# S4D convolution beside a gated linear unit: squarings two at a time, another order in the preparation, other stores

## The chip, the cores and the metric

The kernel runs on one core of one Trainium2 chip. The metric is the device time of one execution in microseconds (us); the time before the change is the median of three runs, 716.96 us. The engines are named as in the profile: PE is TensorE, DVE is VectorE, ACT is ScalarE, POOL is GpSimd and SP is SyncE, which issues most DMAs.

## The reference

The input x is 1 x 2048 x 448 (L positions, D channels), N = 256 modes per channel, and the hidden width of the gated unit is 1792. All is fp32.

```python
xn = (x - mean) / sqrt(var + 1e-5)                   # over the channels
dt = exp(log_dt); A = -exp(log_A_real) + 1j*A_imag; C = (C_real + 1j*C_imag) * dt
P  = exp((A*dt)[:, :, None] * arange(L))             # D x N x L
K  = 2 * einsum("dn,dnl->dl", C, P).real
y  = irfft(rfft(xn.T, 2L) * rfft(K, 2L))[:L].T + xn * D_skip
h  = sigmoid(xn @ w_gate) * (xn @ w_up)
out = x + y + h @ w_down
```

## The kernel before, in words

Two Python generators write the program: `conv` (L1016), the long convolution, and `glu` (L727), the gated unit. A loop at the end (L1106 to L1125) takes the next piece from the one that is behind by its planned share of the work (`WP`, `WX`, `WK`, `WS` are planned costs). The tile framework then schedules the instructions of each engine; `tc.issue_after(ins)` keeps an instruction behind `ins` in that order, and `hp` gives priority. Each engine runs its own row of instructions in order.

The gated unit. The hidden width is cut in 14 pieces of 128, and positions in tiles of 512. An fp32 product is done as three products of high and low parts (`xh`, `xl`; `wh`, `wl`; `hh`, `hl`; `dh`, `dl`). For each piece and tile `gate` (L692) makes two halves `gu` in PSUM (L706, 12 matmuls each), ACT makes `th` (L714), DVE `hf` from `th` and the second half (L717), ACT `hh` (L722), DVE `hl` (L724). So hf is what frees the banks of `gu`. DVE also makes `wl` from the loaded weights (L760). After a group of pieces the down projection `po` runs (L819) and DVE adds it into `acc` (L824). The banks with the tag "gu" are four, in turn, for gate halves, `po`, `kq` and the transposes of x (L212), whose low parts DVE takes out as `xl` (L222) and `xr` (L225); `xr` holds the last 64 channels, high and low.

The convolution's stages:
- Layer norm (statistics L248 to L263, `xn` L270) and transposes, to about 30 us.
- `prep` (L342), run as two generators for the two halves of the channels: `exp` (L304) with the fractions `fr` (L312, L313) and a polynomial `pl` (L317), reciprocals in pieces of 128 columns (`pieces`, L321 to L323), `m`, `w`, `s` (L368 to L372). A round of both generators is placed behind the hf that is `LAG` = 3 hfs back. The layer norm statistics of the second 8 blocks of x stand in the program ahead of these rounds, behind `xls[0]`, the instruction that makes `xr` of the second tile of x. `x_spec` (matmuls L281) makes spectra of x between rounds.
- `kgen` (L458), 107 to 535 us: 56 chunks of 8 channels in 7 groups of 8. Per chunk PE makes phases `tr` (L539), ACT sines `S` (L545 to L548), POOL multiplies magnitudes `me`, `mf` (L517) out of powers `pm`, ACT squares some (L530), DVE makes `Et` (two products, L599 and L600) and `Ft` (L601), and PE multiplies them into `ko` (64 matmuls, L613). `powers` (L446) makes the `pm` of the next group: ten squarings on DVE (L453), three copies with 1 added on ACT (L451, L456). It is called once a group, at its chunk c = 4, behind the Ft of the chunk before.
- `spectra` (L841), 535 to 700: products with tables (`there`, `back`, L900 and L927), and inverse transforms `last(h, m)` (L960) that DVE adds into the outputs (L968). h is the half of the channels; m = 0, 2, 4, 6 stands for pairs of blocks of both halves of the output. They are interleaved with the end of the gated unit.

Stores: `out` (L234) writes four blocks of half width for four partition groups, each on the next of the queues of SP, ACT and POOL in turn. The first two quarters of the output lie in `ac`, the last two in `accs[2]` and `accs[3]`. In the last group of the gated unit `last(1, 0)` and `last(1, 2)` come ahead of the third block of the second tile, `last(1, 4)` and `last(1, 6)` behind the fourth.

## Time and profile before

| | |
|---|---|
| runs | 716.56, 716.96, 721.07 us; median 716.96 |
| profiled execution | 717.89 us; span 716.1 us; mean granted clock 0.98 |
| PE busy | 671.3 us, 94% |
| DVE busy | 550.8 us, 77% |
| ACT busy, POOL busy | 428.7 us, 378.8 us |
| DMA | 117.22 MB, mean 164 GB/s |

The profile is of one execution. The span runs from its first instruction to its last; the execution's own time has 1.8 us more. A row of the time line has the start in us, the busy time in us, the engine, the line, the operation with output and inputs, and how many were put together; in square brackets stands the engine's idle time just before, and what ended it. Rows of one engine overlap a little, since they are pipelined, so what one costs is better seen from start to start. A row of the table by windows has busy time (and count of instructions) of PE, PE's weight loads, DVE, ACT and POOL, then the clock granted to PE as a share of full speed, the DMA share and GB/s. Line numbers are those of the kernel before, unless rows of the order after are shown, whose numbers differ by 1 to 5.

### The profile page before, as it was taken

Reading aid. Unit: us, or ns where it says so; the run is one execution under the profiler, and the core shown is the slowest. Engines: PE = TensorE matmul, PEld = TensorE weight load, DVE = VectorE, ACT = ScalarE, POOL = GpSimd, SP = SyncE. Lnnn points to the kernel's source line nnn. Section 1 sums busy time; section 2 is a strip of 40 time slices with the busy share of each in tenths; the row PEclk is TensorE's granted clock in tenths of the full one; section 3 lists DMA queues with packets and bytes.
Section 4 is the critical chain, followed back from the end, with each engine's and each line's share of the span. In section 5 each row is a group of like instructions: output and inputs, shape, how many; then the busy total and the mean of one; then the engine's idle time right before and its main releaser. Section 6 shows DMA issues by size and latency. Waiting matters only on the chain.

```text
span 716.1 us, 19096 instructions
## 1 busy us (share of the span) xinstructions
PE 671.3 (94%) x7752; PEld 528.2 (74%) x7752; DVE 550.8 (77%) x766; ACT 428.7 (60%) x678; POOL 378.8 (53%) x431
## 2 busy tenths in 40 slices
PE   3898999999997998999999999999989999999995
PEld 2676888878876885656878778887867777776784
DVE  5899997599889889898588988987936555556543
ACT  3656974588687689996578778678643322313320
POOL 2101138556987978797368688598954002351002
PEclk9998999999999898999999999999999999999998
DMA  9947174464254444556933333242259988999645
GB/s 204 235 145 231 50 230 132 145 198 136 63 169 148 138 111 127 160 164 196 274 107 101 95 110 116 68 147 57 57 173 309 242 234 239 264 281 222 182 131 154
DMA packets 93991, 117.22 MB, mean 164 GB/s; under 512 B 12240, under 2 KB 77776, under 8 KB 93904
## 3 DMA queue, kind: packets, MB, share of 16 engines
q1 hardware_dynamic: 65904, 91.87, 45.6%
q10 hardware_dynamic: 25424, 18.24, 8.8%
q0 software_dynamic: 2576, 5.90, 2.9%
q8 instruction: 61, 1.00, 0.6%
q14 instruction: 26, 0.21, 0.1%
HBM read 72.13 MB, written 43.84 MB: 162 GB/s over the span
## 4 chain that ended last, share of the span: by engine, by line
PE 71%; DVE 13%; ACT 4%; issue 3%; SPq 3%; DMA 3%; POOL 1%; ACTq 0%; POOLq 0%; DVEq 0%
PE gu L706 29%; PE po L819 17%; PE sp L900 7%; PE ko L613 6%; PE pv L927 4%; PE tr L539 4%; SPq L489 2%; DVE Et L599 1%; PE gu L281 1%; DVE Ft L601 1%; DVE Et L600 1%; DMA acc<-in_A_u_dram 1%; DMA ph<-ph_d 1%; DVE pm L453 1%; DVE hl L724 1%
## 5 line engine op out<-in xcount | busy, mean ns | idle before, releaser
L517 POOL TENSOR_TENSOR me<-me,pm 128x32 f32<-128x32 f32 (+1 forms) x168 | 145.1, 864 | 67.6 <-DVE Et L600 56.8
L517 POOL TENSOR_TENSOR mf<-mf,pm 128x64 f32<-128x64 f32 (+1 forms) x112 | 121.3, 1083 | 6.1
L706 PE MATMUL gu<-xh,wh 128*128 128x512 f32 x336 | 100.5, 406 | 0.7 <-ACT xh L221 0.7
L706 PE MATMUL gu<-xh,wl 128*128 128x512 f32 x336 | 96.2, 393 | 0.0
L706 PE MATMUL gu<-xl,wh 128*128 128x512 f32 x336 | 96.1, 392 | 0.0
L600 DVE TENSOR_TENSOR Et<-me,S 128x1024 f32<-128x1024 f32 x56 | 79.7, 1423 | 14.4 <-ACT me L530 14.0
L599 DVE TENSOR_TENSOR Et<-me,S 128x1024 f32<-128x1024 f32 x56 | 79.1, 1414 | 14.3 <-ACT S L548 13.6
L819 PE MATMUL po<-dh,hh 128*128 128x448 f32 x224 | 85.0, 379 | 2.9 <-DVE hf L717 2.9
L601 DVE TENSOR_TENSOR Ft<-mf,S 128x1024 f32<-128x1024 f32 x56 | 80.1, 1430 | 6.5 <-PE ko L613 4.0
L819 PE MATMUL po<-dl,hh 128*128 128x448 f32 x224 | 83.1, 371 | 0.0
L819 PE MATMUL po<-dh,hl 128*128 128x448 f32 x224 | 81.8, 369 | 0.0
L545 ACT ACTIVATE S<-tr 128x1024 f32<-128x1024 f32 x56 | 57.9, 1034 | 37.8 <-PE tr L539 36.1
L613 PEld LDWEIGHTS ko<-Et,Ft 128*32 128x32 f32 x3584 | 55.5, 112 | 30.6 <-issue 13.6
L706 PEld LDWEIGHTS gu<-xh,wh 128*128 128x128 f32 x336 | 61.7, 191 | 19.8 <-issue 4.4
L613 PE MATMUL ko<-Et,Ft 128*32 128x64 f32 x3584 | 66.5, 224 | 9.4 <-DVE Ft L601 7.4
L722 ACT CAST hh<-hf 128x512 fp32r<-128x512 f32 x56 | 35.0, 625 | 65.6 <-DVE hf L717 58.3
L706 PEld LDWEIGHTS gu<-xh,wl 128*128 128x128 f32 x336 | 63.4, 189 | 14.4 <-DVE hf L717 0.7
L706 PEld LDWEIGHTS gu<-xl,wh 128*128 128x128 f32 x336 | 63.4, 189 | 13.5
L783 POOL TENSOR_TENSOR dl<-rd,dh 128x448 fp32r<-128x448 f32 x14 | 26.2, 1871 | 83.5 <-ACT dh L782 83.5
L548 ACT ACTIVATE S<-S,hpi 128x1024 f32<-128x1024 f32 x56 | 65.7, 1174 | 0.0
L824 DVE SCALAR_TENSOR_TENSOR acc<-po,acc 128x448 f32<-128x448 f32 x80 | 48.0, 615 | 21.1 <-PE po L819 21.0
L717 DVE SCALAR_TENSOR_TENSOR hf<-th,gu 128x512 f32<-128x512 f32 x56 | 38.0, 679 | 32.1 <-PE gu L706 24.5
(208 smaller groups left out, 1302.1 us busy)
## 6 DMA issues: line engine op xcount, KB each, us to landing
sk_d<-sk ACTq DMA_DIRECT2D x14, 512.0 KB
sx<-x_d SPq DMA_DIRECT2D x32, 224.0 KB
skl<-sk_d SPq DMA_DIRECT2D x16, 448.0 KB
vp<-v_d SPq DMA_DIRECT2D x16, 448.0 KB
v_d<-vt SPq DMA_DIRECT2D x14, 448.0 KB
ph<-ph_d SPq DMA_DIRECT2D x224, 24.0 KB
wt_d<-wh SPq DMA_DIRECT2D x9, 512.0 KB
wt_d<-wl SPq DMA_DIRECT2D x9, 512.0 KB
```

The costliest lines, as they stand in the source:

```text
L517: ins = nc.gpsimd.tensor_tensor(m[:, :, w + a : 2 * w : n], m[:, :, a:w:n], par(base + i).unsqueeze(2).to_broadcast([128, 4 * DC, w // n]) ...
L545: nc.scalar.activation(rows(cs), pv, AF.Abs)
L548: sins[:] = [nc.scalar.activation(cs, cs, AF.Sin, scale=-TWO_PI, bias=hpi)]
L599: v.tensor_tensor(Et[:, :, :, 32:64], two(me[:, :, 32:64]), S[:, 1::-1], ALU.mult)
L600: v.tensor_tensor(Et[:, :, :, 0:32], two(me[:, :, 0:32]), S[:, 1:3, :, ::-1], ALU.mult)
L601: fts[:] = [v.tensor_tensor(Ft, two(mf), S[:, 3:5], ALU.mult)]
L613: mm = nc.tensor.matmul(ko[32 * j : 32 * j + 32, sl], Ft[:, cc, DC * h + 4 * q + j], Et[:, cc, DC * h + 4 * q + j], start=(k == 0), stop=( ...
L706: glu_mm[:] = [nc.tensor.matmul(ps, a_, b_, start=(n == 0), stop=(n == len(mm) - 1))]
L717: marks[1] = v.scalar_tensor_tensor(hf, th, 1.0, pgu[1], ALU.add, ALU.mult)
L819: glu_mm[:] = [nc.tensor.matmul(po, a_[:, bs], w_, start=(n == 0), stop=(n == 3 * fc - 1))]
L824: v.scalar_tensor_tensor(acc[:, b], po, 0.5, acc[:, b], ALU.mult, ALU.add)
L900: mm = nc.tensor.matmul(to, tb[:kk, t, 64 * c : 64 * c + 64], rhs, start=True, stop=True, skip_group_check=True,)
```

## The change

Three things are changed; what is computed is not.

**Squarings.** `powers` takes a list of the squarings to make, and is called at chunks c = 1 to 6 of a group instead of once at c = 4: two squarings a chunk by a table of numbers, at c = 6 all three ACT copies and no squaring. Each call stands behind the Ft of the chunk before.

**Preparation.** The first two rounds of `prep` (exponent clamp, fractions) are as before; rounds after the second are also behind `xls[0]`, and the statistics of the second 8 blocks come after the third round, behind `frs[0]`, the last of the fractions (L313). `x_spec` comes one round later.

**Stores.** `out` is given the queues, the columns and the number of blocks. The first half of the columns of `ac` and of `accs[2]` goes on POOL's queue only, the second on SP's and ACT's. In the last group `last(1, 4)` and `last(1, 6)` come ahead of the fourth block of the second tile instead of behind it, with stores of `accs[2]`'s second half and of blocks 12 to 14 at full width; after the fourth block only block 15 is stored.

```diff
+PWS = [(), (1, 2), (3, 4), (5, 7), (8, 9), (10, 11), (12,)]
...
-    def out(src, b0, h):
-        ds = slice(H * h, H * h + H)
+    def out(src, b0, nb, ds, engs):
         for g in range(4):
-            eng = (nc.sync, nc.scalar, nc.gpsimd)[outs[0] % 3]
-            outs[0] += 1
-            eng.dma_start(blocks(out_t, g, b0, 4)[:, :, ds], src[32 * g : 32 * g + 32, :, ds])
+            eng = engs[g % len(engs)]
+            eng.dma_start(blocks(out_t, g, b0, nb)[:, :, ds], src[32 * g : 32 * g + 32, b0 % 4 : b0 % 4 + nb, ds])
...
-        v.scalar_tensor_tensor(fr, ki, -ln2l, fr, ALU.mult, ALU.add)
+        frs[:] = [v.scalar_tensor_tensor(fr, ki, -ln2l, fr, ALU.mult, ALU.add)]
...
-    def powers(pms, g, behind=None):
+    def powers(pms, g, js=range(1, 13), behind=None):
...
-        with tc.issue_after(behind.ins) if behind else nullcontext():
-            nc.scalar.activation(pm[:, 0], w, AF.Identity, bias=one)
-        for j in (1, 2, 3, 4, 5, 7, 8, 9, 10, 11):
-            v.scalar_tensor_tensor(pm[:, j], w, 2.0, w, ALU.add, ALU.mult)
-            w = pm[:, j]
-        for o in (slice(1, 6), slice(7, 12)):
-            nc.scalar.activation(pm[:, o], pm[:, o], AF.Identity, bias=one)
+        for j in js:
+            if j in (6, 12):
+                continue
+            src = w if j == 1 else pm[:, j - 2 if j == 7 else j - 1]
+            v.scalar_tensor_tensor(pm[:, j], src, 2.0, src, ALU.add, ALU.mult)
+        if js[-1] == 12:
+            with tc.issue_after(behind.ins) if behind else nullcontext():
+                nc.scalar.activation(pm[:, 0], w, AF.Identity, bias=one)
+                for o in (slice(1, 6), slice(7, 12)):
+                    nc.scalar.activation(pm[:, o], pm[:, o], AF.Identity, bias=one)
...
-                if c == 4 and NCH * (g + 1) < NCK:
+                if 0 < c < 7 and NCH * (g + 1) < NCK:
                     with tc.issue_after(fts[0].ins):
-                        powers(pms, g + 1, sins[0])
+                        powers(pms, g + 1, PWS[c], sins[0])
...
-                        if final and (t, b) == (1, 2):
+                        if final and t == 1 and b >= 2:
                             sp_mm[:] = glu_mm
-                            for m in (0, 2):
+                            for m in (4 * b - 8, 4 * b - 6):
                                 lasts[0](1, m)
+                            if b == 3:
+                                out(accs[2], 8, 4, slice(H, D), (nc.sync, nc.scalar))
+                                out(accs[3], 12, 3, slice(0, D), (nc.sync, nc.scalar))
...
-                    if final:
-                        out(acc, 8 + 4 * t, 0)
-                if final:
-                    sp_mm[:] = glu_mm
-                    for m in (4, 6):
-                        lasts[0](1, m)
-                    for t in range(2):
-                        out(accs[2 + t], 8 + 4 * t, 1)
+                    if final and t == 0:
+                        out(acc, 8, 4, slice(0, H), (nc.gpsimd,))
+                    elif final:
+                        out(acc, 15, 1, slice(0, D), (nc.sync, nc.scalar))
...
-                    out(ac[:, 4 * q : 4 * q + 4], 4 * q, h)
+                    out(ac[:, 4 * q : 4 * q + 4], 4 * q, 4, ds, (nc.sync, nc.scalar) if h else (nc.gpsimd,))
...
-                with tc.issue_after(xls[0].ins):
-                    for b in range(8):
-                        x_stats(sm, 8 + b, xes[b // 4][:, b % 4])
-                x_scales(sm, 8, 8)
...
                     for p in list(preps):
                         try:
-                            with tc.issue_after(hfs[max(0, len(hfs) - LAG)].ins):
+                            behind = tc.issue_after(xls[0].ins) if n > 1 else nullcontext()
+                            with tc.issue_after(hfs[max(0, len(hfs) - LAG)].ins), behind:
                                 next(p)
...
+                    if n == 2:
+                        with tc.issue_after(frs[0].ins):
+                            for b in range(8):
+                                x_stats(sm, 8 + b, xes[b // 4][:, b % 4])
+                        x_scales(sm, 8, 8)
...
-                    if n in (2, 3):
+                    if n in (3, 4):
```

What stands in DVE's row at three places. First, from the second hf on (about 29.6 us before): the fractions `fr`, the low parts `xl` and `xr`, and the first statistics. Before:

```order
L717 SCALAR_TENSOR_TENSOR hf<-th,gu 128x512
L312 SCALAR_TENSOR_TENSOR fr<-ki,ex 112x514 x2
L222 TENSOR_TENSOR xl<-tr,xh 128x512
L313 SCALAR_TENSOR_TENSOR fr<-ki,fr 112x514
L222 TENSOR_TENSOR xl<-ko,xh 128x512
L313 SCALAR_TENSOR_TENSOR fr<-ki,fr 112x514
L222 TENSOR_TENSOR xl<-kp,xh 128x512
L225 TENSOR_TENSOR xr<-gu,xr 64x512
L248 BN_STATS st_84<-xe_116 128x6 x4
```

and after:

```order
L719 SCALAR_TENSOR_TENSOR hf<-th,gu 128x512
L223 TENSOR_TENSOR xl<-tr,xh 128x512
L223 TENSOR_TENSOR xl<-ko,xh 128x512
L223 TENSOR_TENSOR xl<-kp,xh 128x512
L226 TENSOR_TENSOR xr<-gu,xr 64x512
L311 SCALAR_TENSOR_TENSOR fr<-ki,ex 112x514 x2
L726 TENSOR_TENSOR hl<-hf,hh 128x512
L312 SCALAR_TENSOR_TENSOR fr<-ki,fr 112x514 x2
L247 BN_STATS st_84<-xe_116 128x6 x4
```

The four passes for the fractions went from ahead of `xr` to behind it.

Second, some rows on, from the fourth hf back to the reciprocals. Before, from the fourth hf:

```order
L717 SCALAR_TENSOR_TENSOR hf<-th,gu 128x512
L368 SCALAR_TENSOR_TENSOR m_379<-a_377,b_378 112x512
L370 TENSOR_TENSOR w_380<-a_377,b_378 112x512
L372 TENSOR_TENSOR s_381<-a_377,b_378 112x512
L368 SCALAR_TENSOR_TENSOR m_391<-a_389,b_390 112x512
L370 TENSOR_TENSOR w_392<-a_389,b_390 112x512
L372 TENSOR_TENSOR s_393<-a_389,b_390 112x512
...
L323 RECIPROCAL m_379<-m_379 112x128 x2
L724 TENSOR_TENSOR hl<-hf,hh 128x512
L323 RECIPROCAL m_379<-m_379 112x128 x2
L323 RECIPROCAL m_391<-m_391 112x128
```

and after, up to the fourth hf (the third stands 16 rows ahead of it):

```order
L367 SCALAR_TENSOR_TENSOR m_361<-a_359,b_360 112x512
L369 TENSOR_TENSOR w_362<-a_359,b_360 112x512
L726 TENSOR_TENSOR hl<-hf,hh 128x512
L322 RECIPROCAL m_349<-m_349 112x128 x4
L371 TENSOR_TENSOR s_363<-a_359,b_360 112x512
L255 TENSOR_SCALAR ve<-mv 128x8
L316 SCALAR_TENSOR_TENSOR pl<-pl,fr 112x514 x2
L322 RECIPROCAL m_361<-m_361 112x128 x4
L719 SCALAR_TENSOR_TENSOR hf<-th,gu 128x512
```

The fourth hf stood ahead of `m`, `w`, `s` and all eight reciprocals, and stands behind them now; the fifth hf followed the reciprocals before.

Third, a stretch of `kgen` in the first group. Before, the burst at c = 4:

```order
L601 TENSOR_TENSOR Ft<-mf_1102,S_1103 128x1024
L453 SCALAR_TENSOR_TENSOR pm_1167<-W_108 128x128
L453 SCALAR_TENSOR_TENSOR pm_1167<-pm_1167 128x128 x3
L724 TENSOR_TENSOR hl<-hf,hh 128x512
L453 SCALAR_TENSOR_TENSOR pm_1167<-pm_1167 128x128 x2
L600 TENSOR_TENSOR Et_1105<-me_1109,S_1107 128x32x32
L453 SCALAR_TENSOR_TENSOR pm_1167<-pm_1167 128x128
L717 SCALAR_TENSOR_TENSOR hf<-th,gu 128x512
L453 SCALAR_TENSOR_TENSOR pm_1167<-pm_1167 128x128
L599 TENSOR_TENSOR Et_1105<-me_1109,S_1107 128x32x32
L453 SCALAR_TENSOR_TENSOR pm_1167<-pm_1167 128x128
```

and after, behind the Ft of two chunks:

```order
L603 TENSOR_TENSOR Ft<-mf_1108,S_1107 128x1024
L453 SCALAR_TENSOR_TENSOR pm_1110<-W_108 128x128
L453 SCALAR_TENSOR_TENSOR pm_1110<-pm_1110 128x128
L601 TENSOR_TENSOR Et_1104<-me_1109,S_1103 128x32x32
L602 TENSOR_TENSOR Et_1104<-me_1109,S_1103 128x32x32
L719 SCALAR_TENSOR_TENSOR hf<-th,gu 128x512
L603 TENSOR_TENSOR Ft<-mf_1108,S_1103 128x1024
L726 TENSOR_TENSOR hl<-hf,hh 128x512
L453 SCALAR_TENSOR_TENSOR pm_1110<-pm_1110 128x128 x2
```

The squarings stand two behind each Ft; the rows of Et, Ft, hf and hl between them are in much the same order.

More of the change, by code (lines that the diff above doesn't have):

```diff
@@ L1068, in conv @@
                 preps = [prep(pst, h, srcs[h]) for h in range(2)]
-                with tc.issue_after(xls[0].ins):
-                    for b in range(8):
-                        x_stats(sm, 8 + b, xes[b // 4][:, b % 4])
-                x_scales(sm, 8, 8)
-                p01 = pst.tile([CP, 2, 2, 2 * N], F32R, name="p01", tag="xe0")
-                for i in range(2):
-                    slots[f"P{i}"] = p01[:, i]
-                x1ab = pst.tile([128, 2, 2, D], F32, name="x1ab", tag="xe1")
-                slots["x1a"], slots["x1b"] = x1ab[:, 0], x1ab[:, 1]
                 n = 0
@@ L1088, in conv @@
                             preps.remove(p)
+                    if n == 2:
[3 more added lines that the diff above has]
+                        x_scales(sm, 8, 8)
+                        p01 = pst.tile([CP, 2, 2, 2 * N], F32R, name="p01", tag="xe0")
+                        for i in range(2):
+                            slots[f"P{i}"] = p01[:, i]
+                        x1ab = pst.tile([128, 2, 2, D], F32, name="x1ab", tag="xe1")
+                        slots["x1a"], slots["x1b"] = x1ab[:, 0], x1ab[:, 1]
                     yield WP
                     n += 1
-                    if n in (2, 3):
-                        if n == 2:
+                    if n in (3, 4):
+                        if n == 3:
                             slots["x1c"] = pst.tile([128, 2, D], F32, name="x1c", tag="raw1")
                         for b in range(0, 4, 2):
-                            yield from x_spec([xns[n - 2][:, b + i] for i in range(2)], 4 * (n - 2) + b)
+                            yield from x_spec([xns[n - 3][:, b + i] for i in range(2)], 4 * (n - 3) + b)
             with tc.tile_pool(name="pk", bufs=1, side="right", reuse_waits="tile") as pk:
@@ L1106, in s4d_glu_kernel @@
     turns = []
-    lasts, glu_mm, sp_mm, glu_on, outs, x1s, hfs, xls = [], [], [], [], [0], [0], [], []
+    lasts, glu_mm, sp_mm, glu_on, x1s, hfs, xls = [], [], [], [], [0], [], []
     xq, psc, raws, acl, marks, slots, pqs = list(x_first), [], [], [], [None, None], {}, []
-    W1s, GGs, act, exps = [], [], [], []
+    W1s, GGs, act, exps, frs = [], [], [], [], []
     gens = [conv(), glu()]
```

## The prediction

> **What bounds the kernel now.** I read the page's first block, then what TensorE (PE) waited for, then the table by stage, and last the time line around each longer wait.

> The page: the span and the busy time by engine.
> ```profile
> span 716.1 us, 19096 instructions
> PE 671.3 (94%) x7752; PEld 528.2 (74%) x7752; DVE 550.8 (77%) x766; ACT 428.7 (60%) x678; POOL 378.8 (53%) x431
> ```
> PE's waits (total, times, longest), and three stages of the table by windows.
> ```profile
> PE tr L212 <- DVE xn L270: 12.4, 1, 12.4
> PE ko L613 <- DVE Ft L601: 7.4, 5, 3.4
> PE po L819 <- DVE hf L717: 2.9, 1, 2.9
> PE gu L281 <- DVE hf L717: 2.8, 1, 2.8
> PE gu L706 <- DVE xr L225: 2.8, 1, 2.8
> ```
> ```profile
> core 0: us, PE busy (x) PEld busy (x) DVE busy (x) ACT busy (x) POOL busy (x), PEclk, DMA share, GB/s
> 150.00:240.00 90.00, 84.56 (x1244) 68.53 (x1243) 83.04 (x87) 70.92 (x102) 74.21 (x72) 0.96 0.43 132
> 240.00:330.00 90.00, 85.06 (x1290) 59.74 (x1290) 82.58 (x89) 76.01 (x121) 74.99 (x79) 0.96 0.48 146
> 535.00:700.00 165.00, 163.97 (x1248) 124.54 (x1246) 89.86 (x177) 45.13 (x86) 32.08 (x39) 1.00 0.87 233
> ```
> PE is the bound: of 44.8 us without a matmul, 12.4 are the start, before xn exists, and the end costs some more. In the middle VectorE (DVE) is nearly as full, 92% in 150 to 330, and each longer wait of PE is for DVE. After 535 PE is full, so nothing is to be had there but at the very end. Four waits of 2.75 us or more remain: xr, then hf, in the preparation; Ft, then hf, in the generation of the kernels.

> Such a wait costs more than its idle time. Here is the Ft wait, and the granted clock (the third number from the end) around it:
> ```profile
> 231.39 1.92 PE L613 MATMUL ko<-Et,Ft 128*32 128x64 f32 x62 [3.40 <-DVE Ft L601]
> ```
> ```profile
> 229.00:230.00 1.00, 0.00 (x0) 0.00 (x0) 1.00 (x1) 1.00 (x3) 1.00 (x2) 0.97 1.00 323
> 236.00:237.00 1.00, 1.00 (x4) 0.76 (x4) 0.96 (x1) 1.00 (x3) 1.00 (x1) 0.61 0.21 58
> 237.00:238.00 1.00, 1.00 (x6) 0.84 (x5) 0.00 (x0) 1.00 (x2) 1.00 (x2) 1.00 0.25 59
> ```
> The gap runs from 227.99 to 231.39. The clock is whole until the end of the first row, and back in the last: at half speed from about 229.9 to 236.7. From 231.39 to 236.7 PE did 5.3 us of work at half rate: about 2.6 us lost on top of 3.40.

> **Part 1: low parts of x ahead of the fractions, statistics later.** DVE from the second hf on, and PE where it waited:
> ```profile
> 30.22 1.29 DVE L312 SCALAR_TENSOR_TENSOR fr<-ki,ex 112x514 f32<-112x514 int32 x2
> ...
> 34.54 0.68 DVE L225 TENSOR_TENSOR xr<-gu,xr 64x512 fp32r<-64x512 f32 x1
> 35.26 3.79 DVE L248 BATCH_NORM_STATS2 st<-xe 128x6 f32<-128x448 f32 x7
> ...
> 42.45 0.65 DVE L717 SCALAR_TENSOR_TENSOR hf<-th,gu 128x512 f32<-128x512 f32 x1
> ...
> 47.43 0.68 DVE L717 SCALAR_TENSOR_TENSOR hf<-th,gu 128x512 f32<-128x512 f32 x1
> ...
> 53.60 1.76 DVE L323 RECIPROCAL m<-m 112x128 f32<-112x128 f32 x2
> ...
> 58.30 1.16 DVE L760 TENSOR_TENSOR wl<-wraw,wh 128x1024 fp32r<-128x1024 f32 x1
> ...
> 61.86 1.23 DVE L317 SCALAR_TENSOR_TENSOR pl<-pl,fr 112x514 f32<-112x514 f32 x2
> ...
> 63.08 0.68 DVE L717 SCALAR_TENSOR_TENSOR hf<-th,gu 128x512 f32<-128x512 f32 x1
> ```
> ```profile
> 35.28 0.72 PE L706 MATMUL gu<-xr,wh 128*128 128x512 f32 x1 [2.75 <-DVE xr L225]
> ...
> 55.76 0.96 PE L706 MATMUL gu<-xh,wh 128*128 128x512 f32 x3
> ...
> 63.81 0.74 PE L819 MATMUL po<-dh,hh 128*128 128x448 f32 x1 [2.91 <-DVE hf L717]
> ```
> ```profile
> 38.00:39.00 1.00, 1.00 (x4) 0.80 (x3) 1.00 (x3) 0.00 (x0) 0.00 (x0) 0.60 0.35 61
> ```
> Four fraction passes of about 0.6 us (1.29 for two) go behind xr, so xr ends 2.4 us sooner. The wait shrinks from 2.75 to about 0.35, and with it goes the half clock behind it (back at 0.60 of the stretch from 38 to 39, so half from 35.1 to about 38.5, of which 35.3 to 38.5 was work: 1.6 lost). PE is 4.0 us earlier from there.

> Then the price. The fourth hf, at 47.43 ahead of all reciprocals, now stands behind all eight of them. Third hf: the same work ahead plus one BN row (0.6) less a few, so 42.6. Between it and the fourth stand eight reciprocals (1.76 for two, 6.9 for all, since they overlap a little), four pl (2.5), six sums and differences m, w, s and one hl of nearly the same shape (0.6 each, 4.2), wl (1.16) and statistics (0.6): 15.4. The fourth hf ends at 42.6 + 0.6 + 15.4 + 0.6 = about 58.6 (before: 48.1). The gate product that takes over the PSUM bank it frees ran at 55.76; with one group of spectrum products (0.94) no longer ahead and 4.0 us gained, PE is there at 50.8. It waits 7.8 us, longer than any wait removed, and loses about 2.5 more at half clock (3.41 us of it if the clock comes back in one period as at 35.1 to 38.5, 6.83 if as at 229.9). The old hf wait at 63.81 then goes: the fifth hf ends near 65.3 (6.2 us of rows after the fourth: wl, two w, four pl, two ci, hl), and PE, 5.1 us of work past the long wait plus 2.5, comes at 66.2. Before, PE left that place at 63.81 and lost 2.7 to the clock, so 66.5 counted whole. On these rows part 1 is 0.3 better; the sixth hf, though, comes about 1.8 later than before, and one weight cast on ACT is now ahead of an hh that PE needs. I take +2.0 (ends −2 and +8).

> The eight later statistics rows cost DVE nothing new; they are moved. One preparation round ends one hf earlier, at a place where none of PE's longer waits lies, so nothing.

> **Part 2: squarings two at a time.** All ten squarings of a group used to come behind one Ft:
> ```profile
> L453 DVE SCALAR_TENSOR_TENSOR pm<-pm x63: 277/400/1171, 107.3 to 451.0; 128x128 f32<-128x128 f32 x63
> ...
> 200.00 1.51 DVE L600 TENSOR_TENSOR Et<-me,S 128x1024 f32<-128x1024 f32 x1 [2.42 <-ACT me L530]
> ...
> 212.96 4.31 DVE L453 SCALAR_TENSOR_TENSOR pm<-pm 128x128 f32<-128x128 f32 x6
> ...
> 230.05 1.28 DVE L601 TENSOR_TENSOR Ft<-mf,S 128x1024 f32<-128x1024 f32 x1
> ```
> ```profile
> 220.49 0.83 ACT L456 ACTIVATE pm<-pm,one 128x640 f32<-128x640 f32 x1 [2.13 <-DVE pm L453]
> ```
> ```profile
> 281.50 1.76 PE L281 MATMUL gu<-xt,wx 32*64 32x448 f32 x4 [2.81 <-DVE hf L717]
> ```
> ```profile
> 281.00:282.00 1.00, 0.50 (x2) 0.29 (x4) 1.00 (x2) 1.00 (x2) 0.92 (x2) 0.57 0.00 0
> 287.00:288.00 1.00, 1.00 (x18) 0.32 (x12) 0.75 (x1) 0.48 (x2) 0.92 (x2) 0.52 0.65 215
> ```
> Ten take about 5.5 us (0.4 in the median, six at 212.96 took 4.31). By the late Ft at 230.05 all ten are issued in both orders; what changes is that six of them come one to three chunks sooner, four of these ahead of 206, where DVE stood idle (2.42 at 200.00). Those four are worth about 2.2 us, and ACT no longer stands waiting between two copies (2.13 at 220.49) ahead of the sines that Et takes. So the 3.40 comes to about 1.4, and no wait of up to 1.49 was followed by half clock: 2.0 + 2.6 = 4.6. The hf wait at 281 lies in the next burst in the same way: 2.0 and its clock (0.57 in 281 to 282, 0.52 still in 287 to 288; 6.83 us, 3.1 lost), 5.1. Together 9.7. Against it stand the chunks that get the squarings: of the five Ft waits (7.4 in all) the others are 0.7 or so, at chunks already on the edge, and a pair there (1.1) goes straight to PE where nothing else covers it. Six groups with three such chunks, a fifth of them on the edge: about 3.7. Net −6.0. The ends: −12.5 (both waits with their clock gone, 3.40 + 2.6 + 0.70 + 2.81 + 3.1), and +2 (nothing gained, two pairs on the path).

> [...]

> **Part 3: stores.** The end of PE, the last stores, and the windows behind:
> ```profile
> 705.72 1.74 PE L960 MATMUL pv<-vp,wf 64*32 64x224 f32 x64
> 706.47 3.56 SPq L240 DMA_DIRECT2D out_dram<-acc  x4
> 706.79 2.21 DVE L968 TENSOR_TENSOR acc<-acc,pv 128x448 f32<-128x448 f32 x4 [0.35 <-PE pv L960]
> ```
> ```profile
> 712.00:714.00 2.00, 0.00 (x0) 0.00 (x0) 0.00 (x0) 0.00 (x0) 0.00 (x0) 0.50 0.45 152
> ```
> From the last matmul's end at 707.5 to the end are 8.6 us, with data moving into 712 to 714. Now the inverse transforms come ahead of the last po block, so that after PE's end stand one add of DVE (0.6) and one full-width block instead of four adds (2.21) and half pieces in three queues. But the same bytes leave in the last microseconds, so I take −1 (ends −2 and +0.5: nine po matmuls no longer cover the transforms' adds). First halves on POOL alone: eight and four issues instead of a third, under 0.9 each (SP's four take 3.56), beside a PE that is 163.97 of 165 busy and a POOL busy 32.08: nothing, ends 0 and +1 if the last down-weight cast behind them came late.

> **Sum.** 717.89 (the profiled execution: its span and 1.8 around) + 2.0 − 6.0 − 1.0 = 712.9. That execution was 0.93 above the median 716.96, so 712.0 for the median.

> **Rivals.** (a) DVE has the room and both waits in the generation go with their clock: −12.5 + 0.5 − 1 gives 704. For it: 2.42 and more idle ahead of the late Ft; against: 92% busy. (b) Slower: the fourth hf behind the reciprocals. If the wait is 9 rather than 7.8, the clock is lost for 6.83 us of work (3.4) and the sixth hf brings a second wait of 3 with its clock (2.7), part 1 is +8 (18.1 less the 9.96 that go: 2.75 + 1.6 + 2.91 + 2.7); the delayed gate then leaves DVE no room in part 2, and the time is 716.96 + 8 − 1 = 724. It decides once the fourth hf ends later than PE's arrival by about 3 us more than the 2.75 and 2.91 that go. For it: DVE had no idle time from 30.22 to the fifth hf, in the rows shown or those left out; against: the 63.81 wait goes too. (c) The spreading does nothing, since the sum ahead of the late Ft is the same: 716.96 + 2 − 1 = 718.

> **Numbers.** Forecast 0.33, (a) 0.27, (c) 0.18, (b) 0.22. One per cent, 7.2 us, is about what a measurement of this kernel can tell from no change. Faster by over that (below 709.8): (a) and a tenth of the forecast's case, 0.30; within it: the rest of the forecast and (c), 0.48; slower (above 724.1): (b), 0.22, whose time lies at that bound. The range takes in −2 −12.5 −0.5 at the low end (702) and +8 +2 −1 at the high end (726).

> **What would show it.** Right: xr's wait below 0.5, a wait of 7 to 8 us near 51 to 58 for hf and none at 64; no clock below 0.9 in 220 to 240 and 280 to 290, ACT's pm copies waiting for nothing; 7.5 us or so from PE's end to the end. Wrong: no wait near 51 to 58 (then the order does not bind there and the time is some 4 lower), new Ft or hf waits over 2.75 in 110 to 450, or a store queue whose last piece lands later than now.

## The result, and the profile after

The median of 20 runs is 724.36 us (718.7 to 725.68), against 719.06 of 20 runs of the kernel before: the ratio is 1.006, with a 95% interval of 1.0043 to 1.0078. The change makes the kernel slower by 0.6%. The forecast was 712.0, 0.7% faster; the measured time lies in its range of 702 to 726, on the other side of no change.

The page, and what TensorE (PE) waited for, in the kernel after:
```profile
span 722.5 us, 19096 instructions
PE 675.8 (94%) x7752; PEld 528.8 (73%) x7752; DVE 559.6 (77%) x766; ACT 428.0 (59%) x678; POOL 376.4 (52%) x433
```
```profile
PE gu L708 <- DVE hf L719: 6.9, 1, 6.9
PE ko L615 <- DVE Ft L603: 3.6, 4, 2.4
PE ko L615 <- DVE Et L601: 2.8, 2, 2.6
PE gu L280 <- DVE xl L220: 1.9, 1, 1.9
PE gu L280 <- DVE hf L719: 1.6, 2, 1.1
PE ko L280 <- ACT x1c L295: 1.3, 1, 1.3
```
Of the four long waits of before (2.75 for xr, 2.91 and 2.81 for hf, 3.40 for Ft) none is left as it was; one of 6.9 is new.

To place the loss I compare where both kernels stand at rows that each has once: the first of the products `kp` (L563 before, L565 after), early in the generation, and the last group of them, at its end. Before they start at 171.99 and 529.48, after at 180.50 and 538.44. So 8.5 us are lost ahead of the first, 0.5 between them, and from the second to the end of the span 2.6 are won (186.6 and 184.1): together the 6.4 by which the spans differ.

Here is the first stretch in the kernel after: PE, then VectorE (DVE), then ScalarE (ACT).
```profile
32.95 0.50 PE L708 MATMUL gu<-xr,wh 128*128 128x512 f32 x1 [0.35 <-DVE xr L226]
...
58.22 1.65 PE L708 MATMUL gu<-xh,wh 128*128 128x512 f32 x3 [6.94 <-DVE hf L719]
...
65.96 0.47 PE L824 MATMUL po<-dh,hh 128*128 128x448 f32 x1 [1.07 <-DVE hf L719]
...
70.76 0.60 PE L280 MATMUL tr<-xn,wx 32*64 32x448 f32 x4
...
76.49 0.98 PE L280 MATMUL tr<-xn,wx 32*64 32x448 f32 x8 [0.28 <-ACT x1ab L293]
...
79.99 0.97 PE L280 MATMUL ko<-xn,wx 32*64 32x448 f32 x4 [1.30 <-ACT x1c L295]
...
87.49 0.87 PE L708 MATMUL gu<-xh,wh 128*128 128x512 f32 x3
```
```profile
57.55 0.62 DVE L719 SCALAR_TENSOR_TENSOR hf<-th,gu 128x512 f32<-128x512 f32 x1
...
65.23 0.67 DVE L719 SCALAR_TENSOR_TENSOR hf<-th,gu 128x512 f32<-128x512 f32 x1
...
70.40 0.68 DVE L719 SCALAR_TENSOR_TENSOR hf<-th,gu 128x512 f32<-128x512 f32 x1
```
```profile
77.08 1.28 ACT L375 ACT_TABLE_LOAD   x1
...
79.43 0.51 ACT L295 COPY x1c<-ko 128x448 f32<-128x448 f32 x1
```
The fourth, fifth and sixth hf come at 57.55, 65.23 and 70.40. PE waits 6.94 for the fourth. Behind the sixth, PE still has two of the four groups of spectrum products (L280), from 70.76 and from 76.49 on. The last is done in pieces and waits for ACT to copy the group before it out of PSUM (0.28 and 1.30); ACT had loaded a table (1.28 us from 77.08) ahead of the second of these copies. The second group's first gate product is at 87.49. Here are the same two groups and this product before:
```profile
54.82 0.60 PE L281 MATMUL tr<-xn,wx 32*64 32x448 f32 x4
...
59.49 0.60 PE L281 MATMUL tr<-xn,wx 32*64 32x448 f32 x4
...
80.22 0.94 PE L706 MATMUL gu<-xh,wh 128*128 128x512 f32 x3
```
There they took 0.94 each, ahead of PE's wait for the fifth hf (2.91 at 63.81), so they filled time that would otherwise have been waiting.

From 28 us to the first `kp`, PE's idle time is 11.2 us, against 6.6 before; the half clock loses 4.6 in both; the rest, 3.8 of the 8.5, is longer time for the same rows, 1.4 of it in the spectrum products, which ran side by side before (the last 16 started between 59.49 and 59.97) and in pieces now (eight from 76.49, four from 79.99, four from 80.43).

The end of the kernel after: the last matmul, the last add and the last stores.
```profile
714.80 4.41 SPq L239 DMA_DIRECT2D out_dram<-acc  x6
715.84 0.62 DVE L829 SCALAR_TENSOR_TENSOR acc<-po,acc 128x448 f32<-128x448 f32 x1 [0.54 <-PE po L824]
```
```profile
715.44 0.37 PE L824 MATMUL po<-dh,hl 128*128 128x448 f32 x1
```
From the last matmul's end, 715.8, to the end are 6.7 us, against 8.6 before.

### The profile page after: what moved, and what is told of

The parts are those of the page before. It is cut to its first block, busy times and chain, and to the rows that moved or that the text cites. A ratio compares the mean times of both kernels' runs of the same rounds, so it can differ in the third digit from the quotient of the medians.

```text
span 722.5 us, 19096 instructions
## 1 busy us (share of the span) xinstructions
PE 675.8 (94%) x7752; PEld 528.8 (73%) x7752; DVE 559.6 (77%) x766; ACT 428.0 (59%) x678; POOL 376.4 (52%) x433
## 5 line engine op out<-in xcount | busy, mean ns | idle before, releaser
L519 POOL TENSOR_TENSOR me<-me,pm 128x32 f32<-128x32 f32 (+1 forms) x168 | 147.3, 877 | 76.6 <-DVE Et L602 46.3
L519 POOL TENSOR_TENSOR mf<-mf,pm 128x64 f32<-128x64 f32 (+1 forms) x112 | 118.0, 1053 | 5.3
L708 PE MATMUL gu<-xh,wl 128*128 128x512 f32 x336 | 97.9, 396 | 0.0
L601 DVE TENSOR_TENSOR Et<-me,S 128x1024 f32<-128x1024 f32 x56 | 81.2, 1451 | 10.9 <-ACT S L550 9.6
L602 DVE TENSOR_TENSOR Et<-me,S 128x1024 f32<-128x1024 f32 x56 | 80.8, 1442 | 5.9 <-ACT me L532 4.1
L716 ACT ACTIVATE th<-gu 128x512 f32<-128x512 f32 x56 | 33.6, 600 | 53.3 <-PE gu L708 52.8
L829 DVE SCALAR_TENSOR_TENSOR acc<-po,acc 128x448 f32<-128x448 f32 x80 | 48.1, 615 | 19.7 <-PE po L824 19.6
```

The costliest lines, as they stand in the source:

```text
L519: ins = nc.gpsimd.tensor_tensor(m[:, :, w + a : 2 * w : n], m[:, :, a:w:n], par(base + i).unsqueeze(2).to_broadcast([128, 4 * DC, w // n]) ...
L601: v.tensor_tensor(Et[:, :, :, 32:64], two(me[:, :, 32:64]), S[:, 1::-1], ALU.mult)
L602: v.tensor_tensor(Et[:, :, :, 0:32], two(me[:, :, 0:32]), S[:, 1:3, :, ::-1], ALU.mult)
L708: glu_mm[:] = [nc.tensor.matmul(ps, a_, b_, start=(n == 0), stop=(n == len(mm) - 1))]
L829: v.scalar_tensor_tensor(acc[:, b], po, 0.5, acc[:, b], ALU.mult, ALU.add)
```

## The experiments

Fifteen kernels ran; the text calls them by the first part of their labels. The table has the ratio to the kernel before with its interval, and from the profile how much later than in the kernel before (171.99, 529.48, span 716.1) the two rows and the end come, in us.

| kernel | ratio | first kp | last kp | span |
|---|---|---|---|---|
| the change | 1.0060 (1.0043 to 1.0078) | +8.5 | +9.0 | +6.4 |
| p_squarings_alone | 0.9991 (0.9967 to 1.0015) | −0.6 | −1.0 | +1.6 |
| x_order_alone | 1.0255 (1.0223 to 1.0287) | +8.1 | +18.9 | +20.8 |
| s_stores_alone | 0.9949 (0.9926 to 0.9972) | −1.1 | −2.6 | −5.3 |
| f1_recip_behind_hf4 | 1.0077 (1.0047 to 1.0107) | +8.0 | +9.8 | +6.9 |
| x1_low_parts_first | 1.0135 (1.0091 to 1.0179) | +0.3 | +7.2 | +8.0 |
| xsp_spectra_later | 1.0166 (1.0112 to 1.0221) | +5.2 | +11.4 | +13.9 |
| b1_recip_behind_hf5 | 1.0066 (1.0032 to 1.0100) | +3.1 | +3.6 | +4.3 |
| x1f2_both | 1.0139 (1.0093 to 1.0186) | +7.4 | +8.5 | +9.0 |
| sp_squarings_stores | 0.9941 (0.9914 to 0.9969) | −0.2 | −1.7 | −3.9 |
| px_squarings_order | 1.0134 (1.0103 to 1.0166) | +10.1 | +8.5 | +11.7 |
| anr_two_reciprocals | 1.0007 (0.9984 to 1.0030) | +4.8 | +5.5 | +3.7 |
| spool_pool_helps | 0.9983 (0.9961 to 1.0005) | +1.6 | −0.2 | −2.4 |
| spd_idle_filled | 1.0109 (1.0078 to 1.0140) | −0.3 | +9.9 | +8.4 |
| ad_idle_filled | 1.0238 (1.0204 to 1.0271) | +8.5 | +20.4 | +18.3 |
| spx1_low_parts_too | 0.9996 (0.9976 to 1.0015) | +2.0 | +1.4 | −1.2 |

The spans are one execution each; the ratios are of many, and decide.

**The three parts, each alone.** Each kernel has one part of the change's diff on the kernel before: `PWS` and `powers`; or the loop of the preparation with the statistics and `x_spec`; or `out` with its calls.

> The kernel before with the squarings two at a time (and the three copies at c = 6), nothing else. Theory 1 (the loss is all in the preparation's order; the squarings only move the waits of TensorE from some chunks to others): within 2 us of the kernel before, with the 3.40 us Ft wait near 231 shrunk by at least 1 us and other Ft or Et waits of 1 to 3 us in its place. Theory 2 (the squarings, each pair ahead of an Et, are on the path and cost): 3 to 6 us slower, and nothing lost before 107 us. Theory 3 (the forecast's part 2): 4 to 8 us faster, both waits and their half clock gone.

```diff
-                if c == 4 and NCH * (g + 1) < NCK:
+                if 0 < c < 7 and NCH * (g + 1) < NCK:
```

The ratio is that of no change, as theory 1 had it; theory 3, the forecast's, is out. The late Ft's wait has fallen, by 1.0, and that for hf at 281 by 0.8, with the wait for xl behind it:
```profile
228.50 1.10 PE L617 MATMUL ko<-Et,Ft 128*32 128x64 f32 x64 [2.40 <-DVE Ft L605]
...
275.36 0.97 PE L282 MATMUL gu<-xt,wx 32*64 32x448 f32 x4 [0.76 <-DVE hf L721]
...
279.51 1.75 PE L282 MATMUL gu<-xt,wx 32*64 32x448 f32 x4 [1.25 <-DVE xl L220]
...
318.81 0.86 PE L617 MATMUL ko<-Et,Ft 128*32 128x64 f32 x42 [2.60 <-DVE Et L603]
```
```profile
279.00:280.00 1.00, 0.49 (x2) 0.29 (x4) 1.00 (x3) 1.00 (x3) 1.00 (x2) 0.50 0.00 0
289.00:290.00 1.00, 1.00 (x6) 0.78 (x4) 0.00 (x0) 0.00 (x0) 0.92 (x2) 0.92 0.00 0
```
The 2.81 at 281 is now 0.76 and 1.25. Yet the clock (third number from the end) is at half from 279 to 289, after waits no longer than these, and a wait of 2.60 for an Et is new. A gate product that started at 277.85 in the kernel before starts at 273.29 here, 4.6 us sooner, but one that started at 355.58 starts at 355.61. From first to last kp, PE's idle time is 15.4 us (16.1 before) and the loss to half clock 6.5 (5.9 before).

> The kernel before with the preparation's order alone (low parts of x ahead of the fractions, statistics later, spectrum products a round later). Theory 1: the whole loss, 6 to 9 us slower, with a wait of 6.5 to 7.5 us for the fourth hf near 51 to 58 and the first gate product of the second group 7 to 8 us later than before (79.9 before). Theory 2 (the squarings cost, the order is even): within 1.5 us of before. If stages behind take part of the loss back, as the kernel's other waits leave room, 3 to 6 us slower.

```diff
-                    if n in (2, 3):
+                    if n in (3, 4):
```

It costs 8.1 us to the first kp, as theory 1 had it, and then another 10.8 in the generation, which no theory had: it is 2.55% slower, four times the whole change's 0.6%. In 250 to 360 the waits are longer than before, for instance this one, 2.81 before:
```profile
292.82 1.75 PE L281 MATMUL gu<-xt,wx 32*64 32x448 f32 x4 [5.68 <-DVE hf L717]
```

> The kernel before with the other stores and the inverse transforms ahead of the last block, nothing else. Theory 1: 1 to 2 us faster, the time from the last matmul's end to the end 8.6 before and 6.5 to 7.5 now. Rival (the same bytes leave on the same engines, so only issue time is saved): within 0.5 us.

```diff
-                    if final:
-                        out(acc, 8 + 4 * t, 0)
+                    if final and t == 0:
+                        out(acc, 8, 4, slice(0, H), (nc.gpsimd,))
```

Faster by 0.5%, 3.7 us, rather more than expected. From the last matmul's end to the end are 6.6 us, 2.0 less than before. The rival is out. Some of the rest is a little earlier: between last kp and the end, kernels with the old stores take 186.6 to 189.8 us, those with the new ones 183.8 to 185.1. The kernel before has 0.85 us of waits around 650 that the stores alone have not. In four others with the old stores (p, x, xsp, px) stands a wait of 2 us or more there that none with the new stores has; here it is in p:
```profile
647.52 1.01 PE L904 MATMUL sp<-skl,tb 128*64 128x224 f32 x4 [2.12 <-ACT vt L937]
```
It is for ACT's copies (`vt`), and ACT's queue issues stores of `ac` near there with the old code (two from 640.80 in the kernel before); that these stores are what ACT is late by was not tried by itself. What is left of the 3.7 us, about 1, the runs don't place.

**What in the order costs 8 us.**

> The changed kernel with one number changed: the round of the preparation that holds the reciprocals is placed one hf later, so that the fourth hf stands ahead of all eight reciprocals again, with xr still ahead of the fractions. Theory 1: the wait near 51 to 58 goes; TensorE is 4 us early at the fifth hf, which comes near 63 as before, so a wait of 5 to 7 us stands there; 4 to 6 us faster than the changed kernel, within 2 us of the kernel before. Theory 2 (the squarings cost): no faster than the changed kernel by more than 1.5 us.

```diff
-    with tc.issue_after(hfs[max(0, len(hfs) - LAG)].ins), behind:
+    with tc.issue_after(hfs[max(0, len(hfs) - LAG + (1 if n == 3 else 0))].ins), behind:
```

The wait for the fourth hf goes, and the fifth hf's is longer than expected; then comes one for the spectrum copies:
```profile
64.70 0.74 PE L824 MATMUL po<-dh,hh 128*128 128x448 f32 x1 [8.80 <-DVE hf L719]
...
86.96 0.63 PE L438 MATMUL ko<-ident,pl 112*128 112x112 f32 x2 [2.37 <-ACT x1ab L295]
```
Nothing is won. Theory 1 as I had it, the fourth hf's place as the price, falls.

> The kernel before with one thing: preparation rounds after the second stand behind the instruction that makes xr, so the low parts of x come ahead of the fractions; statistics and spectrum products stay where they were. Theory A (VectorE, with no idle time from 30 to 70, sets when the fifth and sixth hf come, so what TensorE gains at xr it waits for later): the xr wait falls from 2.75 to under 0.5, the wait at the fifth hf grows from 2.91 to 5.5 to 7, and the second group's first gate product starts within 1.5 us of before (79.9); total within 2 us. Theory B (the xr wait is worth its price): 3 to 4 us earlier at 79.9 and in the end.

```diff
+    behind = tc.issue_after(xls[0].ins) if n > 1 else nullcontext()
-    with tc.issue_after(hfs[max(0, len(hfs) - LAG)].ins):
+    with tc.issue_after(hfs[max(0, len(hfs) - LAG)].ins), behind:
```

Theory A as far as the preparation goes: xr's wait is 0.31, and the fifth hf's has grown from 2.91 to 5.17, so that the two together are what they were.
```profile
62.09 0.74 PE L819 MATMUL po<-dh,hh 128*128 128x448 f32 x1 [5.17 <-DVE hf L717]
```
The second group's first gate product comes 1.6 us sooner (78.62 against 80.22), but at the first kp the kernel stands 0.3 us behind. In the generation it loses 6.9 more, against both theories.

> The kernel before with one thing: the spectrum products of x a round later (in rounds 3 and 4 instead of 2 and 3). This also takes the reciprocals ahead of the fourth hf in VectorE's order, since rounds then follow each other sooner. Theory A (the products were TensorE's cover ahead of the hf waits; later they stand behind the last hf of the group): 4 to 8 us later at the second group's first gate product, as much as in the whole order alone. Theory B (what costs is xr or the statistics' move): within 1.5 us of before.

```diff
-                            for b in range(0, 4, 2):
-                                yield from x_spec([xns[n - 2][:, b + i] for i in range(2)], 4 * (n - 2) + b)
+                                yield from x_spec([xns[n - 3][:, b + i] for i in range(2)], 4 * (n - 3) + b)
```

The second group's first gate product comes 3.1 us later (83.32), below the range of theory A but well above theory B's; the first kp 5.2 later. So this one edit makes most of the order's 8.1. It does two things, though: the two groups of spectrum products stand behind the sixth hf, and the reciprocals have come ahead of the fourth, so that PE's long wait is here too:
```profile
58.73 1.65 PE L706 MATMUL gu<-xh,wh 128*128 128x512 f32 x3 [6.24 <-DVE hf L717]
```
In f1 the reciprocals stand between the fourth and the fifth hf, as before, and the first kp is 8.0 late all the same, so their place is not the price. Low parts first (0.3) and later spectra (5.2) add up to 5.5 of the 8.1; the statistics' move was not run alone, so its share, and what the three do to each other, stay open.

> The kernel before with one number: the preparation round with the reciprocals one hf later, so that all eight stand behind the fifth hf. Theory A: the fifth hf comes 6 to 8 us sooner, TensorE's wait of 2.91 at 63.8 goes with its half clock, and the second group's first gate product comes 2 to 5 us sooner; total 1 to 5 us faster. Theory C (the kernels' generation starts later by what the preparation is held back): a new wait of 2 us or more between 90 and 125, and no gain.

```diff
-    with tc.issue_after(hfs[max(0, len(hfs) - LAG)].ins):
+    with tc.issue_after(hfs[max(0, len(hfs) - LAG + (1 if n == 3 else 0))].ins):
```

> The kernel before with the low parts of x ahead of the fractions and the preparation round with the reciprocals two hfs later, so that they stand behind the sixth hf. Theory A: with VectorE's work moved behind the last hf of the group, xr's 2.75 and the fifth hf's 2.91 both go with their half clock: 5 to 9 us sooner at the second group's first gate product, total 3 to 9 us faster. Theory C: a new wait between 90 and 125 takes more than half of it back.

```diff
+    behind = tc.issue_after(xls[0].ins) if n > 1 else nullcontext()
-    with tc.issue_after(hfs[max(0, len(hfs) - LAG)].ins):
+    with tc.issue_after(hfs[max(0, len(hfs) - LAG + (2 if n == 3 else 0))].ins), behind:
```

Both are slower, against theory A; and no wait of 2 us or more is new between 90 and 125, so theory C's reason is not it either. Wherever the reciprocals go, PE waits for what then stands behind them: in the first the sixth hf, in the second an add into `acc` that frees a bank.
```profile
71.03 0.74 PE L819 MATMUL po<-dh,hh 128*128 128x448 f32 x1 [2.92 <-DVE hf L717]
```
```profile
76.70 0.74 PE L819 MATMUL po<-dh,hh 128*128 128x448 f32 x1 [6.86 <-DVE acc L824]
```

> The changed kernel with two of the eight reciprocals (the six others are left out, so the modes' angles come out otherwise): 5.1 us less of VectorE's work ahead of the fourth hf, all else as changed. Theory A (VectorE is the bound of 30 to 80, and TensorE's wait for hf is what it has to do): the wait of 6.94 falls to 1 to 2.5 with its half clock, the second group's first gate product comes 5 to 8 us sooner, and the time falls by 3 to 8 us. Rival (the lateness comes from the spectrum products alone): the wait goes but TensorE waits as long behind, for the copies of the spectra; less than 2 us.

```diff
-        for i in range(0, 2 * N, 128):
-            v.reciprocal(t[:, i : i + 128], t[:, i : i + 128])
+        v.reciprocal(t[:, :128], t[:, :128])
```

Theory A holds in size: with six reciprocals less the wait of 6.94 is 2.08, the second group's first gate product comes 8.5 us sooner than in the changed kernel, the first kp 3.7, and the time is that of the kernel before. This tells what 5.1 us less of DVE's work are worth there, not what the reciprocals' place costs. Of the remaining 4.8 us a good half is a wait for the spectrum copies:
```profile
53.02 0.97 PE L707 MATMUL gu<-xh,wh 128*128 128x512 f32 x3 [2.08 <-DVE hf L718]
...
83.70 0.41 PE L437 MATMUL ko<-ident,pl 112*128 112x112 f32 x2 [2.89 <-ACT x1ab L295]
```

**What the squarings do.**

> The kernel before with the squarings two at a time and the preparation's order, with the old stores. Theory A (parts add up but for the squarings, which in this order remove the long waits of 260 to 350 that the order alone has): 5 to 9 us slower than before, 10 us or so faster than the order alone. Rival (the stores, not the squarings, made up for the order alone): 14 us or more slower than before.

```diff
-                        powers(pms, g + 1, sins[0])
+                        powers(pms, g + 1, PWS[c], sins[0])
```

This differs from the order alone by the squarings only, and from first to last kp it takes 12.4 us less (355.9 against 368.3). The wait of 5.68 at 292 is now
```profile
285.87 0.97 PE L282 MATMUL gu<-xt,wx 32*64 32x448 f32 x4 [0.76 <-DVE hf L721]
```
By the ratios of whole executions (1.0255 and 1.0134) it is 8.7 us less. Theory A: the squarings, not the stores, made up for the generation's loss.

> The kernel before with the squarings two at a time and the other stores, without the preparation's order. Theory A (all that the change loses lies in the preparation's order): faster than before by what the stores alone gave, 2 to 4 us, and 6 to 9 us faster than the changed kernel. Rival (the squarings only pay where the generation starts late): no faster than before.

```diff
+PWS = [(), (1, 2), (3, 4), (5, 7), (8, 9), (10, 11), (12,)]
...
-    def out(src, b0, h):
+    def out(src, b0, nb, ds, engs):
```

0.9941: faster than both kernels of this case, by 4.2 us than the one before. It can't be told from the stores alone (0.9949), so the squarings add nothing that these runs can tell where the order is that of before.

> Squarings and stores, with the low parts of x ahead of the fractions and nothing else of the preparation's order. Theory A (each stage on its own): 1 to 2 us less before 107, as the low parts alone gave, and no loss in the generation now that the squarings come in pairs: 1 to 2 us below squarings and stores. Rival (what the low parts alone lost in the generation, 10 us, comes from where TensorE then stands, squarings or not): 4 to 10 us above.

```diff
+    behind = tc.issue_after(xls[0].ins) if n > 1 else nullcontext()
```

Neither theory as it stood: the generation takes 0.6 us less than before where the low parts alone took 6.9 more (so its loss there goes with the squarings in bursts, as theory A said), but it is 2.0 us late at the first kp, and the whole is 3.9 us above squarings and stores.

> The kernel before with the other stores, and with two products of the preparation per half of the channels (the differences s and the ratio w) on GpSimd, which has 2.0 us of work in 40 to 63, instead of VectorE. Theory A: VectorE has 2.4 us less to do before the sixth hf, the wait of 2.91 at 63.8 shrinks by 1 to 2 us; 1 to 4 us faster than the stores alone. Rival (GpSimd is slow at it and the preparation's later rounds wait for it, or the two engines slow each other): not faster than the stores alone.

```diff
-        v.tensor_tensor(w3, w3, m3, ALU.mult)
-        v.tensor_tensor(s3, a3, b3, ALU.subtract)
+        nc.gpsimd.tensor_tensor(w3, w3, m3, ALU.mult)
+        nc.gpsimd.tensor_tensor(s3, a3, b3, ALU.subtract)
```

The rival: the wait of 2.91 is 3.96, and 2.4 us less to do on DVE bought nothing. DVE's order is another here (`wl`, 1.2 us, stands ahead of the third hf, which comes at 43.69 instead of 42.45), and one of its rows of 8 columns, beside GpSimd's second product, takes 1.21 us instead of 0.16. Which of these ate the 2.4 was not separated.

**The half clock in the generation.**

> Squarings and stores without the preparation's order, and eight full 128-row matmuls more in each of the four places where the second half's spectra are made in the generation (L686; about 2 us of matmul each place at most, their result is written over). Theory D (the squarings' gain is given back as half clock in 280 to 325, since the stretches of 32-row matmuls with waits of 0.6 to 1.25 us count as idle for the clock): the 8.5 us lost to half clock in 250 to 360 fall below 4, and the time is 0 to 4 us lower than without them. Rival (waits alone set the clock): the loss stays at 6.5 to 9, and the time is 2 to 6 us higher.

```diff
+            for _ in range(2):
+                nc.tensor.matmul(pss[g][:, :128], ident, ident, start=True, stop=True)
             x_first_stage(pss[g][:, :D], xns, g)
```

> The changed kernel with the same eight matmuls in each of four places. Theory D: the 5.1 us lost to half clock in 250 to 360 fall below 2, the time 0 to 3 us below the changed kernel's. Rival: the loss stays, 2 to 5 us above.

Theory D's remedy fails, and the times are 12 to 13 us above the kernels without it, beyond the rival's range too. The loss to half clock in 250 to 360 (the idle share of the clock times PE's busy time, summed over windows of 1 us) is 6.8 after 8.5, and 10.2 after 5.1; the 64 recorded passes, 0.16 us each from start to start, are 10 us, and from first to last kp the first of the two takes 11.6 us more than without them. The wait that remains is
```profile
281.30 0.41 PE L213 MATMUL gu<-ident,xt 128*64 128x128 f32 x2 [1.43 <-DVE xl L223]
```
So what the added matmuls don't cure is not told by these two runs; the last section has what the traces say of when the clock falls.

## Why the prediction was wrong, by its own steps

- **Xr and the fourth hf: right.** Forecast: xr's wait 0.35, PE at the fourth hf's place at 50.8, the hf's end at 58.6, a wait of 7.8. Measured: 0.35, 51.3 (58.22 less 6.94), 58.2, 6.94. The terms of the hf's end add up to 59.2, not 58.6, so part of the good fit is luck.
- **"I take +2.0" for part 1: the step that failed.** Measured: 8.5 at the first kp. The sum ended at the fifth hf, where it gave 0.3 better, and up to there it was right: PE left that place at 63.81 before, 66.5 with the lost clock counted, and at 65.96 now, with the clock whole. What lay behind was put at nothing but the 1.8 of the sixth hf and one cast. From there to the second group's first gate product PE takes 21.5 us, against 13.7 before (16.4 less the 2.7 of clock). The two groups of spectrum products behind the fifth hf's place are about 5.4 of these 7.8, with 1.6 of waits for ACT; most of the rest is the half clock behind them (81.1 to 84.5) and a wait of 0.47 for an hh. The sum had counted the spectrum products only as 0.94 us of work no longer ahead of the long wait, not where they went. The run nearest to this term is xsp: 5.2 at the first kp.
- **"PE is 4.0 us earlier from there": right and worth nothing.** In x1 the first group of spectrum products comes at 38.55 instead of 42.53. But DVE has no idle time from 30 to the sixth hf (0.06 us up to 68.06 in the kernel before), so DVE sets when that comes, and what PE wins at xr it waits for at the next hf (x1: 2.75 + 2.91 before, 0.31 + 5.17 then). The prediction's own row said "DVE had no idle time"; it was used for rival (b) only.
- **Part 2, −6.0: failed too.** Alone the squarings give 0.9991 (0.9967 to 1.0015). The two waits shrank by half of what was forecast (3.40 to 2.40 instead of 1.4, 2.81 to 0.76 and 1.25 together). The clock behind the first came back whole, but the half clock from 279 to 289 costs 4.8, where the kernel before lost 3.2, and the new wait of 2.60 for an Et has half clock behind it as well (1.7). "No wait of up to 1.49 was followed by half clock" was true of one trace and is no rule. The price of 3.7 for pairs on the path (its terms give 4.0) did not show as Ft waits: the others over 0.6 are 0.66 and 0.82. Rival (c), nothing gained, is what happened in the order of before. In the order that the change brings the same squarings are worth 8.7 us (px against x), which was not foreseen. That bursts hurt according to where PE stands when they come is a reading of these pairs of runs; no run moved PE's place and nothing else.
- **Part 3, −1: right in sign, too small.** 6.7 against 8.6 us at the end, and 0.85 around 650, where the stores were put at nothing; the stores alone are worth 0.5%.
- **Rival (b)** forecast 724, and 724.36 was measured, but by other terms: it had waits of 9 for the fourth hf and 3 for the sixth, with 6.1 of clock; 6.94 and, for the fifth, 1.07 came, and the clock lost by the first kp is the same as before. That its number fits is luck.

## What to carry to other kernels

Where one engine is full, as DVE was here from 30 us to the sixth hf, a wait of the next engine is that engine's work seen from outside: moving a row ahead of another moved the wait (2.75 and 2.91 before, 0.31 and 5.17 in x1; 8.80 in f1, 2.92 in b1, 6.86 in x1f2). What shortened it was less work for the full engine (5.1 us in anr: 6.94 became 2.08, though 2.4 us in spool did not), and what kept its cost down was other work of the waiting engine ahead of the wait as cover (two groups of spectrum products of 0.94 us before; with them later, in xsp, the first kp came 5.2 late). So of a step that is moved, ask what it was covering where it stood, and what it will have around it where it goes. And test the parts alone and in pairs: here the parts' ratios (0.9991, 1.0255, 0.9949) don't add up to 1.006, and two of the three together, 0.9941, beat the whole.

## What the runs showed of the hardware that was not expected

The granted clock went to half after waits of 0.76 and 1.25 us among matmuls of 32 rows (279 to 289 in the squarings alone), while the same kernel's wait of 2.40 at 228.5 cost no clock. The half-clock stretches were 3.4, 6.8 or 10.2 us long, but for the last one at each kernel's end (6.9 in the kernel before, 5.1 in the kernel after).

The same wait for hf at 281, 2.8 us in the kernel before and in the stores alone, lost 3.2 us of clock in the one and 1.7 in the other, so a single profile's clock loss is good to about 1.5 us a stretch.
